# Block-sparse attention and token mix on one core: the middle value block of a window copied on chip instead of loaded

## The chip, the cores and the metric

The kernel runs on one core of one Trainium2 chip. The metric is the device time of one execution in microseconds (us). A measurement is the median of several runs.

## What is computed

The reference is a block-sparse attention followed by a mixing block. There are 4 batches of 8 heads, 768 positions and 64 values per head; positions are grouped in 24 blocks of 32. Each query block sees its own block and both neighbours, the first and the last block, and three sampled blocks. The first and the last query block see everything.

```python
scores = scale * np.matmul(q, k.transpose(0, 1, 3, 2))
mask = np.abs(blk_i - blk_j) <= window                       # window = 1 block
mask = mask | (blk_i == 0) | (blk_j == 0) | (blk_i == n_blocks - 1) | (blk_j == n_blocks - 1)
for qb in range(n_blocks):
    for kb in sampled_blocks[qb]:
        mask[qb * block:(qb + 1) * block, kb * block:(kb + 1) * block] = True
scores = np.where(mask, scores, -1000000000.0)
attn = np.exp(scores - np.max(scores, axis=-1, keepdims=True))
attn = attn / (np.sum(attn, axis=-1, keepdims=True) + 1e-09)
x = np.matmul(attn, v)                                       # heads side by side: (4, 768, 512)
...
theta = x @ w_theta
yr = np.einsum('ts,bsd->btd', w_tok_r, x * np.cos(theta))
yi = np.einsum('ts,bsd->btd', w_tok_i, x * np.sin(theta))
u = x + yr + yi
return u + np.maximum(u @ w_ch, 0.0)
```

The weights of the mixing block come as 64-bit floats. The kernel decodes them on chip into a high and a low 32-bit part.

## The kernel before

**Two stages.** `attention` comes first and stores its result in device memory (`xs`); `token_mix` reads it back and does the rest. Only a little of the second stage starts inside the first.

**Units.** Attention works on two pairs of batches (`bp` 0 and 1). A pair has six units for its first and last query block (`"w"`, the edges, which see all keys) and then 22 inner units, `i` = 1 to 22, one for each other query block: 56 units in a row, and step `n` of one loop treats several of them at different ages. The order inside a step is written out by hand (lines 483 to 519), and each engine takes its instructions in that order:

- `scores` of unit n+1 on TensorE (`S`, line 333), its row minimum on VectorE (`m`, line 336), the exponentials on ScalarE (`weights`, `P`, line 353);
- `gather_window` and `gather_keys` of unit n+3 on GpSimd: they copy the key blocks that this unit sees into one of two buffers `kg` (lines 293 and 272). A buffer is free when the scores two units earlier are done;
- a share of the decoding of the weights on VectorE and ScalarE (`Decoder`); how many shares a step gets is `due`;
- `turn` and `evict` of unit n (`T`, `pT`), `values` of unit n-1 on TensorE (`X`, line 387), `finish` of unit n-1 on VectorE;
- on SyncE's queue the query load of unit n+6, the window's values of unit n+1 (`load_window`, line 301), the store of the result; on GpSimd the indirect gather of the sampled values of unit n+2 (`gather_values`, line 307); and the next pair's keys, 256 KB at a time.

**The values of a unit.** The product `X` of an inner unit reads two tiles of 128 rows by 1040 (32 rows for each block, all 16 heads of the pair with a column of ones). `va` holds the window: blocks i-1, i and i+1, block b in rows 32 (b mod 3) to 32 (b mod 3) + 31, and the first block in rows 96 to 127. `vb` holds the three sampled blocks, gathered by their row numbers, and the last block. There are two `va`, taken in turn by even and odd units, and four `vb`. Since a `va` was last filled two units ago, one of its three window blocks is still right, and `fresh(i)` lists the two others, i and i+1, as one load of 260 KB or, where they don't lie side by side, two of 130 KB:

```python
for b0, n in fresh(i):
    s0 = 32 * (b0 % 3)
    nc.sync.dma_start(va[s0 : s0 + 32 * n], vr[768 * bp + 32 * b0 : 768 * bp + 32 * (b0 + n)])
```

Block i of unit i also stands in the other `va`, where unit i-1 has it as its own i+1, in the same rows.

**Waits.** Instructions of different engines wait for each other by semaphores, which the framework sets from the tiles that they read and write. A queue is in order: what waits holds up all that stands behind it. In the rows of the order below, `PE_49`, `DVE_49`, `Activation_49` and `Pool_49` count the work of the engines, `DMAHW0` to `7` tell of the landing of transfers from SyncE's and ScalarE's queues, `DMASW0` to `7` of the landing of transfers from GpSimd's. GpSimd's indirect gathers take the eight DMASW semaphores in turn: the gather of unit 1 raises `DMASW0`, that of unit 6 `DMASW5`, that of unit 9 `DMASW0` again.

Of the kernel before, what the change touches and what calls it, by code (L numbers as in the profile page):

```python
# [14 lines left out]
AF = mybir.ActivationFunctionType  # L15
# [4 lines left out]
P = 128  # L20
# [23 lines left out]
class Piece:  # L44
# [6 lines left out]
    def __init__(self, nc, parts, src, name):  # L51
        self.nc, self.parts, self.src, self.name = nc, parts, src, name
        self.f = src.shape[1] // 2
# [73 lines left out]
class Tables:  # L127


    def __init__(self, nc, cp, sampled):  # L130
        self.raw = cp.tile([P, NB * 6], I32, name="sb_raw")
        nc.sync.dma_start(self.raw, sampled.rearrange("i k -> (i k)").partition_broadcast(P))

    def make(self, nc, cp):
        raw = self.raw
# [40 lines left out]
def attention(tc, qT, qE, kT, vr, sampled, xs, ident, early_pieces, late_pieces, first_place, follow, spares):  # L176
# [13 lines left out]
    nc = tc.nc  # L190
    with ExitStack() as ctx, ExitStack() as early:
# [11 lines left out]
        ps_t = ctx.enter_context(tc.tile_pool(name="ps_t", bufs=2, space=PSUM))  # L203
        ps_x = ctx.enter_context(tc.tile_pool(name="ps_x", bufs=2, space=PSUM))


        first = cp.tile([P, 1], F32, name="first")
        nc.vector.memset(first, 0.0)
        tc.keep_in_program_order(nc.scalar.activation(first, first, AF.Exp))
        kgs = [kgp.tile([P, 8, 8, 32], F32, name=f"kg{x}") for x in range(2)]  # L210
        vas = [gp.tile([P, 1040], F32, name=f"va{x}") for x in range(2)]
        vbs = [gp.tile([P, 1040], F32, name=f"vb{x}") for x in range(VB)]
        ks, wide, qbs, qes, unscaled, st, numbers = {}, {}, {}, {}, {}, {}, {}

        def make_places(bp):

            if bp == 0:
                place = first_place([P, 13824], F32, "kv0")
                k = place[:, 0:6144]
                wide[bp] = [place[:, 6144 + 1040 * c : 6144 + 1040 * (c + 1)] for c in range(6)]  # L220
            else:
                k = kp.tile([P, 6144], F32, name="k1")
                wide[bp] = vbs + vbs[:2]
            ks[bp] = k.rearrange("r (s g f) -> r s g f", s=NB, g=8)

        def load_k(bp, s0, n, queue=nc.sync):
            queue.dma_start(ks[bp][:, s0 : s0 + n].rearrange("r s g f -> r s (g f)"), kT[bp][:, s0 : s0 + n])

        def load_wide(bp, t, queue=nc.sync):
            for c in (2 * t, 2 * t + 1):  # L230
                queue.dma_start(wide[bp][c], vr[768 * bp + 128 * c : 768 * bp + 128 * c + 128])

        def load_q(bp, i):
            if i % 2 == 0:
                return
            t = qp.tile([P, 2, 2, 4, 32], F32, tag="q", name=f"q{bp}_{i}", bufs=Q_BUFS)
            nc.sync.dma_start(t.rearrange("r u b p f -> r u (b p f)"), qT[bp][:, i - 1 : i + 1, :])
            qbs[bp, i], qbs[bp, i + 1] = t[:, 0], t[:, 1]
            unscaled[bp, i] = t.rearrange("r u b p f -> r (u b p f)")
# [8 lines left out]
        def scale_edges(bp):  # L248
            scale(qes[bp].rearrange("r b p f -> r (b p f)"))

        def load_edges(bp):
            qes[bp] = ep.tile([P, 2, 4, 64], F32, tag="qe", name=f"qe{bp}")
            nc.sync.dma_start(qes[bp].rearrange("r b p f -> r (b p f)"), qE[bp])


        def number_blocks(bp, i):
# [21 lines left out]
        def fresh(i):  # L278

            runs = []  # L280
            for blk in range(i - 1 if i <= 2 else i, i + 2):
                if runs and blk % 3:
                    runs[-1][1] += 1
                else:
                    runs.append([blk, 1])
            return runs
# [6 lines left out]
                nc.gpsimd.tensor_copy(kgs[i % 2][:, s0 : s0 + n], ks[bp][:, b0 : b0 + n])  # L293

        def load_window(bp, i):
            va = vas[i % 2]
            if i <= 2:
                nc.sync.dma_start(va[96:128], vr[768 * bp : 768 * bp + 32])
            for b0, n in fresh(i):
                s0 = 32 * (b0 % 3)  # L300
                nc.sync.dma_start(va[s0 : s0 + 32 * n], vr[768 * bp + 32 * b0 : 768 * bp + 32 * (b0 + n)])

# [114 lines left out]
        def join(bp, a):  # L417

            xw, f = xws[a], fs[a].rearrange("r t (e b) -> r t b e", e=2)
            for t in range(3):  # L420
                nc.gpsimd.tensor_tensor(xw[:, t], xw[:, t], f[:, t].unsqueeze(3).to_broadcast([P, 2, 2, 65]), op=ALU.mult)
            nc.gpsimd.tensor_tensor(xw[:, 0], xw[:, 0], xw[:, 1], op=ALU.add)
            nc.gpsimd.tensor_tensor(xw[:, 0], xw[:, 0], xw[:, 2], op=ALU.add)

        def joined(bp, a):
            xe = wp.tile([P, 2, 2, 2, 64], F32, tag="xo", name=f"xe{bp}_{a}", bufs=2)[:, 0]
            normalised(f"{bp}_a{a}", xws[a][:, 0], xe)
            for s_ in range(2):
                for z in range(2):
                    r0, p0 = 64 * s_ + 32 * z, 32 * (2 * a + s_)  # L430
                    nc.sync.dma_start(xs[bp, p0 : p0 + 32, (NB - 1) * z].rearrange("r b c -> r (b c)"), xe[r0 : r0 + 32].rearrange("r b e d -> r (b e d)"))

        mxs, fs, xws, xos = {}, {}, {}, {}
        units = []
        for bp in range(NP):
            units += [(bp, "w", (t, a)) for t in range(3) for a in range(2)] + [(bp, i, None) for i in range(1, NB - 1)]
        half = len(units) // 2
# [5 lines left out]
        def do(n, stage, *args):  # L443
            if 0 <= n < len(units):
                stage(units[n], *args)

        def inner(n, stage):
            if 0 <= n < len(units) and units[n][1] != "w":
                stage(*units[n][:2])
# [4 lines left out]
        spares.append(lambda: qp.tile([P, 4, 4, 32], F32, tag="q", name=f"spare{len(spares)}", bufs=Q_BUFS))  # L454
        with tc.manual_schedule():
            tab = Tables(nc, cp, sampled)
            load_edges(0)
            make_places(0)
            load_k(0, 0, 8)
            tab.make(nc, cp)  # L460
            load_wide(0, 0)
            decoder = Decoder(early_pieces + late_pieces, stage, nc.scalar)
            for t in range(1, 3):
                load_k(0, 8 * t, 8)
                load_wide(0, t)
                decoder.load(t - 1, nc.sync)
                load_q(0, 2 * t - 1)
            make_places(1)
            scale_edges(0)
            do(0, scores)  # L470
            do(0, weights)
            steps = len(units) + 1
            for n in range(steps):
                if n == len(units) - 1:
                    early_s.close()
                    next(follow)

                if n <= half:
                    due = 3 * len(early_pieces) * max(n - 3, 0) // (half - 3)
                else:  # L480
                    due = 3 * len(early_pieces) + 3 * len(late_pieces) * (n - half) // (len(units) - 4 - half)
                due = min(due, 3 * len(decoder.pieces)) - decoder.at
                decoder.first_on_scalar(due)
                do(n + 1, scores)
                inner(n + 4, number_blocks)
                inner(n + 3, gather_window)
                inner(n + 3, gather_keys)
                if due > 0:
                    decoder.on_vector()
                if due > 1 and decoder.at % 3:  # L490
                    decoder.on_vector()
                do(n, turn)
                do(n - 1, values)
                if len(units) - 2 <= n < len(units):
                    next(follow)
                do(n, evict)
                do(n + 1, weights)
                inner(n + 3, gather_key)
                inner(n + 3, scale_q)
                decoder.on_scalar()  # L500
                do(n - 1, finish)
                if units[min(n + 6, steps - 2)][:2] not in ((0, 1), (0, 3)):
                    inner(n + 6, load_q)
                inner(n + 1, load_window)
                inner(n - 1, store)
                inner(n + 2, gather_values)
                if 0 < n <= len(units) and units[n - 1][1:] in (("w", (2, 0)), ("w", (2, 1))):
                    join(units[n - 1][0], units[n - 1][2][1])
                if 1 < n <= len(units) and units[n - 2][1:] in (("w", (2, 0)), ("w", (2, 1))):
                    joined(units[n - 2][0], units[n - 2][2][1])  # L510
                if 8 <= n < 20:
                    load_k(1, 2 * (n - 8), 2)
                if n == 24:
                    load_edges(1)
                if n == half - 3:
                    scale_edges(1)
                for t, step in enumerate((half - 2, half, half + 2)):
                    if n == step:
                        load_wide(1, t)

                if n == len(units) - 4:
                    early.close()
                if len(units) - 6 <= n < len(units):
                    next(follow)
            assert not decoder.left(), decoder.left()
# [394 lines left out]
```

## Time and profile before

| | |
|---|---|
| time, median of 3 runs | 618.04 us (616.56 to 621.01) |
| the profiled execution: its time, its span | 618.49 us, 616.7 us |
| granted TensorE clock | 0.955 |
| busy: TensorE, VectorE, ScalarE, GpSimd | 550.4, 413.6, 335.6, 142.1 us |
| moved by DMA | 90.40 MB, mean 147 GB/s |
| GpSimd's gathers of `vb` | 44, issue 1.0 us each, 7.5 us (median) from issue to landing |

In the rows of the profile PE is TensorE, PEld its weight loads, DVE VectorE, ACT ScalarE, POOL GpSimd, SP SyncE; a q behind the name is the engine's queue for transfers and waits. A group's row gives line, engine, operation, out<-in, shape and count, then busy time in us, mean ns of one, and behind the second bar the engine's idle time just before, with what ended it. A row of a window gives, behind its bounds and length, the busy us (and count) of PE, PEld, DVE, ACT and POOL, then the granted clock, the share of time that the 16 DMA engines were busy, and GB/s. A row of the timeline gives start and length in us. The 40 slices of the page are 15.4 us each; a digit is a tenth.

### The profile page before, as it was taken

The numbers are of one execution on the slowest core, as the hardware profiler recorded it, in microseconds if no ns is written. First come the engines' busy times: TensorE is split into PE (matmuls) and PEld (weight loads), VectorE is DVE, ScalarE is ACT, GpSimd is POOL, SyncE is SP. The second block draws the span as 40 slices with busy tenths as digits, with TensorE's granted clock in tenths as the row PEclk, the third lists the DMA queues.
The fourth block names the chain that finished last, engine by engine and source line by source line (L and its number), as shares of the span: only waits on it lengthen the run. The fifth ranks groups of instructions, "written<-read, shape, count | busy, mean of one in ns | idle before, by whom it ended". The sixth has DMA issues, their size and how long they took to land.

```text
span 616.7 us, 17251 instructions
## 1 busy us (share of the span) xinstructions
PE 550.4 (89%) x7072; PEld 438.2 (71%) x7072; DVE 413.6 (67%) x845; ACT 335.6 (54%) x684; POOL 142.1 (23%) x252
## 2 busy tenths in 40 slices
PE   4986759779886886899999997999999999999997
PEld 2755536556654564678888886888888888888886
DVE  5696558679988676777999997446842648723252
ACT  3887468669877676874656645144640346520220
POOL 1496336460584453521101000000000000000000
PEclk9998798899889889899999999999999999999999
DMA  8969899888989899763342222311112210112002
GB/s 321 333 166 263 235 283 264 240 234 299 264 216 279 209 260 247 189 163 119 88 108 81 71 83 78 106 41 35 57 46 78 78 51 21 37 39 78 1 0 103
DMA packets 54095, 90.40 MB, mean 147 GB/s; under 512 B 5504, under 2 KB 31744, under 8 KB 53632
## 3 DMA queue, kind: packets, MB, share of 16 engines
q1 hardware_dynamic: 44480, 58.07, 31.0%
q0 software_dynamic: 6688, 21.78, 13.7%
q10 hardware_dynamic: 2848, 9.44, 5.4%
q8 instruction: 56, 0.92, 0.7%
q14 instruction: 23, 0.19, 0.1%
HBM read 76.68 MB, written 12.58 MB: 145 GB/s over the span
## 4 chain that ended last, share of the span: by engine, by line
PE 56%; DMA 15%; DVE 13%; ACT 6%; issue 5%; POOL 2%; SPq 1%; POOLq 0%; DVEq 0%; ACTq 0%
PE ya L648 14%; DMA va<-in_vr_dram 11%; PE yb L648 7%; PE X L387 6%; PE S L333 4%; PE T L363 4%; PE o L675 3%; PE o L676 2%; PE o L677 2%; PE h L589 2%; PE h L592 2%; PE h L590 2%; ACT zh L630 2%; PE T_w L363 1%; DMA vb<-in_vr_dram 1%
## 5 line engine op out<-in xcount | busy, mean ns | idle before, releaser
L648 PE MATMUL ya<-w_second,zh 128*128 128x512 f32 x288 | 107.1, 396 | 0.0
L648 PE MATMUL yb<-w_second,zh 128*128 128x256 f32 x288 | 80.5, 279 | 0.0
L353 ACT ACTIVATE P<-S,m 128x256 f32<-128x256 f32 x176 | 69.9, 497 | 10.3 <-DVE m L336 10.1
L333 PE MATMUL S<-kg,q 64*32 64x256 f32 x1408 | 59.0, 422 | 17.6 <-issue 14.9
L387 PE MATMUL X<-va,pT 128*32 128x65 f32 (+1 forms) x1408 | 53.3, 241 | 23.4 <-DMA va<-in_vr_dram 17.3
L369 ACT COPY pT<-T 128x512 f32<-128x512 f32 x88 | 48.1, 598 | 45.4 <-PE T L363 44.9
L336 DVE TENSOR_REDUCE m<-S 128x4 f32<-128x1024 f32 x44 | 53.7, 1220 | 28.0 <-PE S L333 27.5
L363 PEld LDWEIGHTS T<-ident,P 128*128 128x128 f32 x352 | 43.7, 155 | 34.1 <-ACT P L353 15.7
L648 PEld LDWEIGHTS ya<-w_second,zh 128*128 128x128 f32 x288 | 54.1, 188 | 14.0
L363 PE MATMUL T<-ident,P 128*128 128x128 f32 x352 | 58.8, 308 | 4.3 <-ACT P L353 3.8
L387 PEld LDWEIGHTS X<-va,pT 128*32 128x32 f32 (+1 forms) x1408 | 38.1, 121 | 33.5 <-issue 16.8
L648 PE MATMUL ya<-w_second,zl 128*128 128x512 f32 x144 | 58.0, 403 | 0.0
L387 PE MATMUL X<-vb,pT 128*32 128x65 f32 (+1 forms) x1408 | 52.7, 240 | 2.6 <-issue 2.6
L648 PEld LDWEIGHTS yb<-w_second,zh 128*128 128x128 f32 x288 | 54.4, 189 | 0.4
L307 POOL DMA_INDIRECT vb<-in_vr_dram,rows x44 | 44.7, 1017 | 30.4 <-PE X_w L387 22.3
L333 PEld LDWEIGHTS S<-kg,q 64*32 64x32 f32 x1408 | 23.8, 114 | 28.6 <-issue 18.2
L387 PEld LDWEIGHTS X<-vb,pT 128*32 128x32 f32 (+1 forms) x1408 | 40.1, 123 | 3.1 <-issue 3.1
L605 DVE SCALAR_TENSOR_TENSOR rr<-t,h 128x512 f32<-128x512 f32 x24 | 16.5, 687 | 37.8 <-ACT t L599 37.8
L648 PE MATMUL yb<-w_second,zl 128*128 128x256 f32 x144 | 40.9, 284 | 0.0
L589 PE MATMUL h<-w_theta_hi,xh 128*128 128x512 f32 x96 | 38.3, 398 | 0.4 <-ACT xh L578 0.4
L683 DVE SCALAR_TENSOR_TENSOR of<-o,xT 128x512 f32<-128x512 f32 (+1 forms) x24 | 13.3, 557 | 36.7 <-PE o L677 33.7
L590 PE MATMUL h<-w_theta_lo,xh 128*128 128x512 f32 x96 | 37.9, 394 | 0.0
(166 smaller groups left out, 1262.9 us busy)
## 6 DMA issues: line engine op xcount, KB each, us to landing
va<-in_vr_dram SPq DMA_DIRECT2D x30, 260.0 KB
q<-in_qT_dram SPq DMA_DIRECT2D x22, 256.0 KB
xs<-xo SPq DMA_DIRECT2D x22, 256.0 KB
xr<-xs SPq DMA_DIRECT2D x22, 256.0 KB
xa<-xs SPq DMA_DIRECT2D x88, 64.0 KB
raw_tok_r<-in_w_tok_r_dram ACTq DMA_DIRECT2D x8, 576.0 KB
out_dram<-of SPq DMA_DIRECT2D x16, 256.0 KB
va<-in_vr_dram SPq DMA_DIRECT2D x30, 130.0 KB
```

The lines of the kernel that those rows point to most:

```text
L307: nc.gpsimd.indirect_dma_start(out=vb[0:96], out_offset=None, in_=vr, in_offset=bass.IndirectOffsetOnAxis(ap=tab.rows[:, bp, i : i + 1], a ...
L333: nc.tensor.matmul(sc[32 * p : 32 * p + 32, e, b, :], q[rows, b, p, :], keys[rows, :, 4 * b + p, :], start=True, stop=True)
L336: nc.vector.tensor_reduce(m.rearrange("r (e b) -> r e b", e=2), sc, axis=AX.X, op=ALU.min)
L353: nc.scalar.activation(pt[:, e, b], sc[:, e, b], AF.Exp, bias=m[:, 2 * e + b : 2 * e + b + 1], scale=-1.0)
L363: nc.tensor.transpose(banks[k // 4][:, k % 4], pt[:, (k // 2) % 2, k % 2, 128 * (k // 4) : 128 * (k // 4) + 128], ident)
L369: nc.scalar.copy(out[:, 4 * h : 4 * h + 4], bank)
L387: nc.tensor.matmul(s["X"][rr, b, e, :], s["T"][0:rows, 4 * c + 2 * e + b, rr], v[0:rows, v0 : v0 + 65], start=c == 0, stop=c == 1,)
L589: nc.tensor.matmul(ps, hi[:, c, :], wh[:, c, :], start=c == 0, stop=False)
L590: nc.tensor.matmul(ps, hi[:, c, :], wl[:, c, :], start=False, stop=False)
L605: nc.vector.scalar_tensor_tensor(r, t, -C1, ps, op0=ALU.mult, op1=ALU.add)
L648: nc.tensor.matmul(acc, z[:, dd], wt[:, t0 : t0 + n], start=first and (n == 512 or c % 2 == 0), stop=last, skip_group_check=n == 256,)
L675: nc.tensor.matmul(ps, wh, uh, start=first, stop=False, skip_group_check=one)
```

## The change

Four things are edited.

1. `load_window`: from unit 3 of a pair on, block i is copied by GpSimd from the other `va` (32 rows by 1040), and only block i+1 is loaded, 130 KB. `gather_values` now stands ahead of `load_window` in the step.
2. The second pair's keys: the same 12 loads of 256 KB, one in every second step from 5 to 27 instead of one in every step from 8 to 19.
3. The decoding in the second half: the six steps after `half` (the second pair's edges) get 4 parts of weight, later steps 7, instead of all the same.
4. At the start, the block numbers and the edge queries are loaded by ScalarE's queue instead of SyncE's, and the first exponential, which brings in its table, stands behind them.

```diff
     def __init__(self, nc, cp, sampled):
         self.raw = cp.tile([P, NB * 6], I32, name="sb_raw")
-        nc.sync.dma_start(self.raw, sampled.rearrange("i k -> (i k)").partition_broadcast(P))
+        nc.scalar.dma_start(self.raw, sampled.rearrange("i k -> (i k)").partition_broadcast(P))
...
         first = cp.tile([P, 1], F32, name="first")
-        nc.vector.memset(first, 0.0)
-        tc.keep_in_program_order(nc.scalar.activation(first, first, AF.Exp))
...
-        def load_edges(bp):
+        def load_edges(bp, queue=nc.sync):
             qes[bp] = ep.tile([P, 2, 4, 64], F32, tag="qe", name=f"qe{bp}")
-            nc.sync.dma_start(qes[bp].rearrange("r b p f -> r (b p f)"), qE[bp])
+            queue.dma_start(qes[bp].rearrange("r b p f -> r (b p f)"), qE[bp])
...
         def load_window(bp, i):
-            va = vas[i % 2]
+            va, runs = vas[i % 2], fresh(i)
             if i <= 2:
                 nc.sync.dma_start(va[96:128], vr[768 * bp : 768 * bp + 32])
-            for b0, n in fresh(i):
+            else:
+
+                runs, slot = [(i + 1, 1)], slice(32 * (i % 3), 32 * (i % 3) + 32)
+                nc.gpsimd.tensor_copy(va[slot], vas[(i + 1) % 2][slot])
+            for b0, n in runs:
                 s0 = 32 * (b0 % 3)
                 nc.sync.dma_start(va[s0 : s0 + 32 * n], vr[768 * bp + 32 * b0 : 768 * bp + 32 * (b0 + n)])
...
             tab = Tables(nc, cp, sampled)
-            load_edges(0)
+            load_edges(0, nc.scalar)
             make_places(0)
             load_k(0, 0, 8)
+
+            nc.vector.memset(first, 0.0)
+            nc.scalar.activation(first, first, AF.Exp)
             tab.make(nc, cp)
...
                 if n <= half:
                     due = 3 * len(early_pieces) * max(n - 3, 0) // (half - 3)
                 else:
-                    due = 3 * len(early_pieces) + 3 * len(late_pieces) * (n - half) // (len(units) - 4 - half)
+
+                    weight = lambda k: 4 * min(k, 6) + 7 * max(k - 6, 0)
+                    due = 3 * len(early_pieces) + 3 * len(late_pieces) * weight(n - half) // weight(len(units) - 4 - half)
...
+                inner(n + 2, gather_values)
                 inner(n + 1, load_window)
                 inner(n - 1, store)
-                inner(n + 2, gather_values)
...
-                if 8 <= n < 20:
-                    load_k(1, 2 * (n - 8), 2)
+                if 5 <= n < 29 and n % 2:
+                    load_k(1, n - 5, 2)
```

How instructions stand on GpSimd, in the steps that gather the values of units 4 to 6 of the first pair. Before (line 307 is the gather, 293 and 272 the key copies):

```order
L307 DMA vb1_121<-in_vr_dram,rows_160 96x1040
L258 TENSOR_LOAD sb_block_136
L293 COPY kg0_116<-kv0_130 128x512 [waits PE_49]
...
L272 COPY kg0_116<-kv0_130 128x256
L307 DMA vb2_122<-in_vr_dram,rows_160 96x1040 [waits DMASW0_49]
L258 TENSOR_LOAD sb_block_136
L293 COPY kg1_117<-kv0_130 128x512 [waits PE_49,Pool_49]
...
L272 COPY kg1_117<-kv0_130 128x256 [waits Pool_49]
L307 DMA vb3_123<-in_vr_dram,rows_160 96x1040 [waits DMASW1_49]
```

And in the change (line 308 is the gather, 299 the new copy, 290 and 269 the key copies):

```order
L308 DMA vb1_119<-in_vr_dram,rows_160 96x1040
L299 COPY va1_117<-va0_116 32x1040 [waits DMAHW3_49,DMAHW1_49,PE_49]
L255 TENSOR_LOAD sb_block_136
L290 COPY kg0_114<-kv0_128 128x512 [waits PE_49]
...
L269 COPY kg0_114<-kv0_128 128x256
L308 DMA vb2_120<-in_vr_dram,rows_160 96x1040 [waits DMASW0_49]
L299 COPY va0_116<-va1_117 32x1040 [waits DMASW3_49,DMASW4_49,DMASW2_49,DMAHW0_49,DMASW1_49,DMAHW7_49,PE_49,Pool_49]
L255 TENSOR_LOAD sb_block_136
L290 COPY kg1_115<-kv0_128 128x512 [waits PE_49,Pool_49]
...
L269 COPY kg1_115<-kv0_128 128x256
L308 DMA vb3_121<-in_vr_dram,rows_160 96x1040
L299 COPY va1_117<-va0_116 32x1040 [waits DMASW5_49,DMAHW7_49,PE_49,Pool_49]
```

Between a gather and the next key copies there is now a copy. The three shown are those of units 3, 4 and 5, whose blocks lie in rows 0, 32 and 64. Each waits for a product on TensorE (`PE_49`) and the landing of the other `va` (`DMAHW`). Those of units 4 and 5 wait for gathers as well: unit 5's for `DMASW5`, which the gather just ahead of it raises, unit 4's for `DMASW1` to `4`, the last of which is the gather just ahead. The same pattern repeats every three units in both pairs: rows 0 without a DMASW wait, rows 32 and 64 with one.

On SyncE, the window's loads of units 5 to 7 (`va1` is the odd units' buffer). Before:

```order
L301 DMA va1_119<-in_vr_dram 32x1040 [waits DMAHW0_49,PE_49]
L301 DMA va1_119<-in_vr_dram 32x1040 [waits DMAHW1_49]
L227 DMA k1_188<-in_kT_dram 128x512 [waits DMAHW2_49]
L237 DMA q0_11_1036<-in_qT_dram 128x512 [waits DMAHW3_49,Activation_49]
L301 DMA va0_118<-in_vr_dram 64x1040 [waits DMAHW5_49,PE_49]
L415 DMA xs_73<-xo0_3_938 128x512 [waits DMAHW6_49,DVE_49]
L227 DMA k1_188<-in_kT_dram 128x512 [waits DMAHW7_49]
L301 DMA va1_119<-in_vr_dram 64x1040 [waits DMAHW0_49,PE_49]
```

And in the change:

```order
L302 DMA va1_117<-in_vr_dram 32x1040 [waits DMAHW1_49,PE_49,Pool_49]
L224 DMA k1_188<-in_kT_dram 128x512 [waits DMAHW2_49]
L234 DMA q0_11_1039<-in_qT_dram 128x512 [waits DMAHW3_49,Activation_49]
L302 DMA va0_116<-in_vr_dram 32x1040 [waits DMAHW5_49,PE_49,Pool_49]
L416 DMA xs_73<-xo0_3_941 128x512 [waits DMAHW6_49,DVE_49]
L302 DMA va1_117<-in_vr_dram 32x1040 [waits DMAHW7_49,PE_49,Pool_49]
```

Each unit has one load of 32 rows now, one of the key loads has gone to another step, and the window's load waits for GpSimd too: for the copy that filled the same rows two units earlier.

## The prediction

> **What bounds the kernel now.** I read the page's slices first, then the windows by stage, then the groups with what ended their idle time, and last the tile that carries the gathered values.
>
> ```profile
> PE   4986759779886886899999997999999999999997
> POOL 1496336460584453521101000000000000000000
> DMA  8969899888989899763342222311112210112002
> 45.00:60.00 15.00, 10.13 (x235) 7.26 (x236) 11.39 (x21) 12.13 (x30) 11.12 (x17) 0.87 1.00 266
> 75.00:90.00 15.00, 11.08 (x332) 7.28 (x316) 10.23 (x21) 12.04 (x29) 7.16 (x13) 1.00 1.00 282
> 400.00:616.00 216.00, 212.58 (x1160) 182.71 (x1158) 108.41 (x204) 74.10 (x114) 0.00 (x0) 1.00 0.15 48
> L387 PE MATMUL X<-va,pT 128*32 128x65 f32 (+1 forms) x1408 | 53.3, 241 | 23.4 <-DMA va<-in_vr_dram 17.3
> ```
>
> There are two programs in one span. From about 275 us on, the token mix keeps TensorE busy (212.58 of 216 us) and the DMA engines nearly idle (0.15); nothing of the change lies there, so that part only moves to where attention ends. In attention it is the other way round: in the two windows the DMA engines are busy all the time (1.00, at 266 and 282 GB/s), TensorE 10 to 11 of 15 us, and its idle time before the window's products is ended mostly by the landing of `va`. GpSimd has about half of its time free. The change takes bytes from the crowded engines and gives work and, as the built order shows, waits to GpSimd's queue. So the question is whether that queue stays off the path.
>
> ```profile
> 47.10 0.92 POOL L307 DMA_INDIRECT vb<-in_vr_dram,rows  x1 [0.16 <-issue]
> 144.23 0.26 PE L387 MATMUL X<-va,pT 128*32 128x65 f32 x4
> ...
> 180.08 1.25 POOL L307 DMA_INDIRECT vb<-in_vr_dram,rows  x1 [0.16 <-issue]
> 274.54 0.26 PE L387 MATMUL X<-va,pT 128*32 128x65 f32 x4
> ...
> 47.10:144.20 97.10, 73.03 (x1946) 51.48 (x1944) 64.38 (x122) 65.21 (x153) 46.51 (x82) 0.88 0.91 253
> POOL kg L293 <- PE S L333: 39.3, 15, 6.2
> ```
>
> These rows are the yardstick. The gather for unit 5 is issued at 47.10 us in the first pair and at 180.08 us in the second; the last unit's value product (unit 22) starts at 144.23 and 274.54 us. The stretches last 97.1 and 94.5 us, 191.6 us together. In the first one GpSimd works 46.5 us, and its idle time is 39.3 us of waiting for TensorE's score products: TensorE leads, GpSimd follows.
>
> **The change part by part.** *Bytes removed.* Forty units (3 to 22 of both pairs) no longer load their middle block.
>
> ```profile
> va<-in_vr_dram SPq DMA_DIRECT2D x30, 260.0 KB
> va<-in_vr_dram SPq DMA_DIRECT2D x30, 130.0 KB
> ```
>
> A block is 130 KB, so 40 x 133,000 bytes = 5.3 MB go. At 266 GB/s that is 20 us of a saturated DMA. It is an upper bound: it counts only while the DMA engines are what is waited for.
>
> *Copies added.* Forty copies of 32 rows by 1040 elements on GpSimd. The nearest rows are its key copies.
>
> ```profile
> L293 POOL COPY kg<-kv 128x512 f32<-128x512 f32 x15 | 9.4, 627 | 26.8 <-PE S L333 26.8
> L293 POOL COPY kg<-kv 128x768 f32<-128x768 f32 x1 | 0.8, 823 | 5.9 <-DVE sb_raw L163 5.9
> ...
> 93.60 0.61 POOL L293 COPY kg<-kv 128x512 f32<-128x512 f32 x1 [5.82 <-PE S L333]
> 94.16 0.74 POOL L272 COPY kg<-kv 128x256 f32 x2
> 95.05 0.96 POOL L307 DMA_INDIRECT vb<-in_vr_dram,rows  x1 [0.15 <-issue]
> ```
>
> 256 more elements in a row cost 0.2 us, so 1040 cost 0.82 + 272 x 0.2/256 = 1.03 us; with the 0.15 us between two GpSimd instructions, 1.2 us. The bounds are 1.0 and 2.1 us (twice, if VectorE gets in its way). From the first key copy to the gather's issue a step takes 1.45 us (93.60 to 95.05), up to 2 us in crowded steps; I take 1.5. The issue itself takes 0.95 us. Without any wait a step of GpSimd would be 1.5 + 0.95 + 1.2 = 3.65 us against 97.1 / 18 = 5.4 us of the pipeline today: hidden.
>
> *The wait added.* This decides. The built order shows that a copy whose slot is at rows 32 or 64 (13 of 20 units in each pair) waits for the landing semaphore of gathers that GpSimd issued before it; for 12 of the 13 that includes the one issued immediately before. Copies into rows 0 to 31 don't. The copy also stands behind the gather in the queue now. So GpSimd issues the gather, stands still until its 390 KB have landed, copies, and only then starts the key copies of two units later and the next gather. Before, it went straight on. What such a landing takes:
>
> ```profile
> DMA to landing us min/median/max: 4.7/7.5/11.6
> DMA to landing us min/median/max: 6.8/9.6/11.6
> DMA to landing us min/median/max: 4.7/5.3/6.2
> DMA to landing us min/median/max: 5.0/5.1/7.6
> 118.00:135.00 17.00, 14.33 (x418) 10.54 (x417) 13.50 (x26) 12.81 (x30) 11.03 (x19) 0.91 0.83 242
> 200.00:233.00 33.00, 27.71 (x744) 19.18 (x735) 24.25 (x47) 23.61 (x56) 16.80 (x31) 0.85 0.88 236
> ```
>
> The four landing rows are of tile `vb`: all gathers, then those of 46 to 62 us (DMA share 1.00), 118 to 135 us and 200 to 233 us, whose shares (0.83 and 0.88) stand below. From issue to landing it is never under 4.7 us, 5.1 to 5.3 where the DMA engines have some air, and 9.6 where they have none. In the changed kernel the same stretch carries 5.3 MB less and lasts longer, so they have air; but the key, query and store transfers of the step go out just when the gather does. Call the landing L; I take 5.6 us, with 4.7 and 7.5 as bounds.
>
> *The sum.* From the gather of unit 5 to the last copy of a pair GpSimd's queue holds: 12 landings that are waited out and a last one before the copy of unit 22, 13 L; 18 copies outside the landings, 18 x 1.2 = 21.6; 16 stretches of key copies, 16 x 1.5 = 24; 5 gathers that nobody waits for, 5 x 0.95 = 4.8. That is 13 L + 50.4, at L = 5.6 us 123.2 us. TensorE's 73 us and the DMA traffic fit beside it, so the queue is the path. Two pairs: 246.4 - 191.6 = +54.8 us. The copy of unit 3 stands before the stretch in each pair: +2.4.
>
> The Trainium skill, page "DMA: Bandwidth & Descriptors", section "Anatomy of one DMA — SWDGE (gpsimd) path", fits such a transfer as 2.0 us plus bytes over 436 GB/s: an estimate of 2.9 us for 399,360 bytes. By it a pair would be 13 x 2.9 + 50.4 = 88 us, less than today's 97, and the wait would cost nothing. No gather in this trace was that fast.
>
> *Smaller parts.* Three thirds of a decoded piece leave the six edge steps of the second pair, where VectorE is nearly full.
>
> ```profile
> 160.00:180.00 20.00, 15.82 (x362) 11.02 (x354) 18.25 (x28) 14.03 (x35) 17.14 (x27) 0.89 0.88 223
> L75 DVE TENSOR_SCALAR ds_tok_r<-da_tok_r 128x576 int32<-128x576 int32 x8 | 5.4, 678 | 0.1
> L77 DVE SCALAR_TENSOR_TENSOR raw_tok_r<-raw_tok_r,ds_tok_r 128x576 f32<-128x576 uint32 x8 | 7.1, 887 | 0.3
> 0.75 0.39 SPq L132 DMA_DIRECT2D sb_raw<-in_sampled_dram  x1
> 1.65 0.43 SPq L227 DMA_DIRECT2D kv<-in_kT_dram  x1
> ```
>
> One third is 0.68 + 0.89 = 1.6 us, three are 4.7; I take -3 (bounds 0 and -4.7), since part lies beside GpSimd's joins. They come back in later steps, under the waits. At the start two transfers go to ScalarE's queue, so SyncE's first key load starts up to 0.9 us earlier; the table load behind them waits for the edge queries anyhow: -0.5 (0 to -0.9). The second pair's keys, 12 loads of 256 KB over 24 steps instead of 12, cost nothing: the last is issued four steps before its use, and each step's share of SyncE's queue gets shorter, not longer. If a step shrank to 3 us the last would still have 12 us. Moving `vb`'s small SyncE loads ahead of `va`'s touches four units of a pair: nothing.
>
> The profiled execution took 618.5 us (span 616.7, and 1.8 around it), 0.5 over the median of 618.0. 618.5 + 54.8 + 2.4 - 3 - 0.5 = 672 us. The half microsecond to the median is far inside the range.
>
> **The rivals.** *The bytes win.* If the waits stayed inside today's idle time of GpSimd, TensorE would find `va` earlier: 618.5 - 20 x 0.9 - 3.5 = 597 us, with 0.9 for the DMA share in the stretch. It needs a pair of units to shrink by 9 us, so 13 L + 50.4 under some 88 us and L under 2.9 us. For it: the DMA share of 1.00 and the 17.3 us waits for `va`. Against it: 4.7 us as the fastest landing. By the skill's fit just named it would happen; the trace does not agree (4.7 to 11.6). Chance 0.06.
>
> *Nothing measurable.* L at about 3.7 us would make a pair 98.5 us, as long as now, and 617 us in all; also where the wait is met early because something else holds the copy just as long. The same minimum speaks against it. Chance 0.04.
>
> *The landings stay as slow as today.* GpSimd's gather then collides with the step's own burst each time, L = 7.5: 2 x 13 x 1.9 = 49 us more, 721 us. For it: the bursts are tied to the same event as the gather. Against: 40 fewer blocks and a longer stretch leave the DMA engines busy some 0.6 of the time (0.9 x 191.6 = 172 us of work less 20, over 246). Chance 0.14.
>
> **How the numbers follow.** The forecast, 672 us, has 0.76. L from 4.7 to 7.2 us alone gives 649 to 714; the small parts and a dearer copy widen it a little: 645 to 715 us. Below lie the first two rivals, above most of the third. About 1% is what a measurement of this kernel can tell from no change. Slower by over 1%: 0.76 + 0.14 = 0.90; within 1%: 0.04; faster by over 1%: 0.06.
>
> **What would show it.** Right: GpSimd's copy of `va` as the largest wait on that engine, ended by the landing of `vb`, some 26 times for 4 to 5 us each; units in a rhythm of two long steps (about 8 us) and a short one (under 4); DMA share in attention near 0.6; TensorE waiting for GpSimd where it waited for `va`; attention ending near 328 us; the token mix unchanged in length. Copies near 1.03 us. Wrong: copies that start right behind the gather's issue, or TensorE still waiting for `va`'s landing. If landings last under 4 us, the term 13 L is mis-sized; if copies take 2 us, the other.

## The result and the profile after

Slower by a tenth. The changed kernel takes 681.34 us (median of 4 runs, 676.56 to 684.5) beside 617.3 us for the kernel before (4 runs, 615.27 to 621.01); the ratio is 1.102 [1.094, 1.111]. The profiled execution is the fastest of the four: 676.56 us, span 674.8, 58.1 us more than the profiled one of before. By the page its granted TensorE clock is 0.921.

The slices and two group rows of the changed kernel's page come first.

```profile
PE   3976766766987576556999999899999999999997
POOL 1394464463376555554600000000000000000000
DMA  8956656656888564646434322221121211102002
L388 PE MATMUL X<-va,pT 128*32 128x65 f32 (+1 forms) x1408 | 55.8, 255 | 80.1 <-POOL va L299 76.4
L299 POOL COPY va<-va 32x1040 f32<-32x1040 f32 x40 | 44.1, 1101 | 110.7 <-DMA vb<-in_vr_dram,rows 95.4
```

In the third line the DMA digits of attention, 8 and 9 before, are mostly 5 and 6 now. The value products (L388) stood idle 23.4 us before, mostly for a transfer; now 80.1 us, 76.4 of them for GpSimd's new copy, so the bytes of `va` are no longer what they wait for. The copy itself (L299) is busy 44.1 us and has 110.7 us of idle time ahead of it, 95.4 of it ended by the landing of `vb`. The row of the waits gives total us, how many, and the longest one, and the row of the tile `vb` the landings.

```profile
POOL va L299 <- DMA vb<-in_vr_dram,rows: 95.4, 22, 6.6
DMA to landing us min/median/max: 4.3/4.8/11.3
```

GpSimd's timeline in the changed kernel shows one period of three units: start, length, and in brackets the idle time before.

```profile
79.98 0.93 POOL L308 DMA_INDIRECT vb<-in_vr_dram,rows  x1
84.66 1.55 POOL L299 COPY va<-va 32x1040 f32<-32x1040 f32 x1 [3.75 <-DMA vb<-in_vr_dram,rows]
86.26 0.74 POOL L290 COPY kg<-kv 128x256 f32<-128x256 f32 x2
86.94 0.74 POOL L269 COPY kg<-kv 128x256 f32 x2
87.84 0.94 POOL L308 DMA_INDIRECT vb<-in_vr_dram,rows  x1
88.78 1.06 POOL L299 COPY va<-va 32x1040 f32<-32x1040 f32 x1
89.78 0.61 POOL L290 COPY kg<-kv 128x512 f32<-128x512 f32 x1
90.33 0.73 POOL L269 COPY kg<-kv 128x256 f32 x2
91.22 0.95 POOL L308 DMA_INDIRECT vb<-in_vr_dram,rows  x1 [0.16 <-issue]
97.03 1.04 POOL L299 COPY va<-va 32x1040 f32<-32x1040 f32 x1 [4.85 <-DMA vb<-in_vr_dram,rows]
```

The copy at 88.78 fills rows 0 to 31 and starts the moment the gather has been issued (87.84 + 0.94). Those at 84.66 and 97.03 go to rows 64 and 32 and stand 3.75 and 4.85 us until the gather just ahead has landed; key copies and the next gather stand behind them.

The two stretches of the yardstick (gather of unit 5 to the last unit's value product) in the changed kernel's timeline and windows:

```profile
51.34 0.93 POOL L308 DMA_INDIRECT vb<-in_vr_dram,rows  x1 [0.16 <-issue]
172.17 0.26 PE L388 MATMUL X<-va,pT 128*32 128x65 f32 x4
207.86 0.99 POOL L308 DMA_INDIRECT vb<-in_vr_dram,rows  x1 [0.16 <-issue]
331.83 0.26 PE L388 MATMUL X<-va,pT 128*32 128x65 f32 x4
51.34:172.20 120.86, 82.31 (x1950) 57.42 (x1949) 64.03 (x122) 65.42 (x153) 60.97 (x92) 0.77 0.63 180
207.86:331.80 123.94, 82.92 (x1936) 58.07 (x1936) 74.20 (x151) 70.74 (x162) 63.52 (x94) 0.81 0.55 154
```

They last 120.8 and 124.0 us where they lasted 97.1 and 94.5. The 58.1 us of the profiled pair split up as follows: start to the first gather of the yardstick 47.10 to 51.34, +4.2; first stretch +23.7; between the stretches 35.85 to 35.69, -0.2; second stretch +29.5; from its end to the span's end 342.2 to 343.0 (616.7 - 274.54, 674.8 - 331.83), +0.8. The token mix only begins later.

### The profile page after: what moved, and what is told of

It is laid out like the page before. It is cut to its first block, busy times and chain, and to the rows that moved or that the text cites. A ratio compares the mean times of both kernels' runs of the same rounds, so it can differ in the third digit from the quotient of the medians.

```text
span 674.8 us, 17347 instructions
## 1 busy us (share of the span) xinstructions
PE 564.4 (84%) x7072; PEld 446.8 (66%) x7072; DVE 414.1 (61%) x845; ACT 335.5 (50%) x684; POOL 182.4 (27%) x292
## 4 chain that ended last, share of the span: by engine, by line
PE 39%; DMA 21%; DVE 12%; POOL 11%; issue 7%; ACT 5%; POOLq 3%; SPq 0%; DVEq 0%
DMA vb<-in_vr_dram,rows 18%; PE ya L654 13%; PE yb L654 7%; POOL kg L269 3%; POOLq L255 3%; POOL kg L290 3%; POOL va L299 3%; PE o L681 2%; PE o L682 2%; PE h L595 2%; PE o L683 2%; PE h L596 2%; PE h L598 2%; ACT zh L636 2%; PE S_w L326 1%
## 5 line engine op out<-in xcount | busy, mean ns | idle before, releaser
L388 PE MATMUL X<-va,pT 128*32 128x65 f32 (+1 forms) x1408 | 55.8, 255 | 80.1 <-POOL va L299 76.4
L388 PEld LDWEIGHTS X<-va,pT 128*32 128x32 f32 (+1 forms) x1408 | 38.1, 129 | 90.5 <-POOL va L299 82.9
L299 POOL COPY va<-va 32x1040 f32<-32x1040 f32 x40 | 44.1, 1101 | 110.7 <-DMA vb<-in_vr_dram,rows 95.4
L334 PE MATMUL S<-kg,q 64*32 64x256 f32 x1408 | 65.2, 490 | 5.4 <-POOL kg L269 4.7
L364 PEld LDWEIGHTS T<-ident,P 128*128 128x128 f32 x352 | 46.2, 163 | 30.8 <-issue 16.7
L654 PEld LDWEIGHTS ya<-w_second,zh 128*128 128x128 f32 x288 | 54.1, 188 | 14.0
L388 PE MATMUL X<-vb,pT 128*32 128x65 f32 (+1 forms) x1408 | 56.1, 255 | 0.3 <-issue 0.3
L395 DVE TENSOR_SCALAR sm<-X 128x4 f32<-128x4 f32 x44 | 7.0, 159 | 73.3 <-PE X L388 73.1
L308 POOL DMA_INDIRECT vb<-in_vr_dram,rows x44 | 43.1, 979 | 16.2 <-PE X_w L388 9.3
L388 PEld LDWEIGHTS X<-vb,pT 128*32 128x32 f32 (+1 forms) x1408 | 41.0, 133 | 0.5 <-issue 0.5
L334 PEld LDWEIGHTS S<-kg,q 64*32 64x32 f32 x1408 | 25.4, 129 | 23.3 <-issue 11.7
```

Of the source, the lines that this page charges most:

```text
L299: nc.gpsimd.tensor_copy(va[slot], vas[(i + 1) % 2][slot])
L308: nc.gpsimd.indirect_dma_start(out=vb[0:96], out_offset=None, in_=vr, in_offset=bass.IndirectOffsetOnAxis(ap=tab.rows[:, bp, i : i + 1], a ...
L334: nc.tensor.matmul(sc[32 * p : 32 * p + 32, e, b, :], q[rows, b, p, :], keys[rows, :, 4 * b + p, :], start=True, stop=True)
L364: nc.tensor.transpose(banks[k // 4][:, k % 4], pt[:, (k // 2) % 2, k % 2, 128 * (k // 4) : 128 * (k // 4) + 128], ident)
L388: nc.tensor.matmul(s["X"][rr, b, e, :], s["T"][0:rows, 4 * c + 2 * e + b, rr], v[0:rows, v0 : v0 + 65], start=c == 0, stop=c == 1,)
L654: nc.tensor.matmul(acc, z[:, dd], wt[:, t0 : t0 + n], start=first and (n == 512 or c % 2 == 0), stop=last, skip_group_check=n == 256,)
```

## Experiments

Two theories stood against each other on the loss. The *landing* theory is the prediction's: a copy of GpSimd into rows 32 or 64 waits for gathers in flight, and that wait is the path. The *copy* theory says that 40 more copies in GpSimd's queue, and products that wait for them, cost it. Later runs ask how much the bytes alone bring and what the start costs. Ratios are to the kernel before on the same chip, with 95% intervals.

**No copy at all.** The middle block is loaded again, as before the change; all else is the change's.

```diff
-            else:
-                runs, slot = [(i + 1, 1)], slice(32 * (i % 3), 32 * (i % 3) + 32)
-                nc.gpsimd.tensor_copy(va[slot], vas[(i + 1) % 2][slot])
```

> Both fresh blocks are loaded again; the other three edits of the change and the place of the gather ahead of the window's load stay. Theory (GpSimd's queue stands still at copies that wait for gathers, and nothing else costs much): back to about 620 us, 617 to 624, the first value product still 3 us later than before because of the start, GpSimd's waits for vb gone. Rival (the respread key loads, the decoding shares or the gather's place cost the most): 640 us or more, attention still ending later than 320 us.

Measured: 618.21 us, 1.0057 [1.002, 1.0095]. With the copy goes nearly the whole loss, although the 5.3 MB are moved again; the order of the gather, the key loads' new steps, the decoding and the start cost at most some 6 us together (0.2 to 0.95%). The waits of this run:

```profile
POOL kg L290 <- PE S L330: 76.7, 32, 7.5
```

GpSimd waits for TensorE's score products again, as before the change. This doesn't part copy from wait; the next ones do.

**The gather behind the copy.** The copies and their waits stay, but the gather just ahead isn't in flight yet.

```diff
-                inner(n + 2, gather_values)
                 inner(n + 1, load_window)
                 inner(n - 1, store)
+                inner(n + 2, gather_values)
```

> The copy stays on GpSimd with its waits, but the gather is issued behind the copy again, so a copy waits for the gather issued one step earlier. Theory: the key copies (1.5 us) and the issue now lie inside the landing, so a waiting step takes about L + 1.35 = 6.2 us instead of L + 2.65 = 7.5, in all 24 x 1.3 = 31 us less: about 647 us, 635 to 658. Rival (the copy's own length and its wait for va set the pace, not the gather's landing): unchanged, 672 to 685 us.

Measured: 643.36 us, 1.048 [1.040, 1.057], as the landing theory had it (647, 635 to 658). The waits of GpSimd's copy, and a stretch of its timeline:

```profile
POOL va L299 <- DMA vb<-in_vr_dram,rows: 50.3, 18, 4.7
81.81 0.94 POOL L308 DMA_INDIRECT vb<-in_vr_dram,rows  x1 [0.16 <-issue]
82.75 0.62 POOL L290 COPY kg<-kv 128x512 f32<-128x512 f32 x1
83.30 0.73 POOL L269 COPY kg<-kv 128x256 f32 x2
85.90 1.05 POOL L299 COPY va<-va 32x1040 f32<-32x1040 f32 x1 [1.86 <-DMA vb<-in_vr_dram,rows]
87.22 0.92 POOL L308 DMA_INDIRECT vb<-in_vr_dram,rows  x1 [0.27 <-POOL va L299]
```

The copy still waits for the gather before it, but that one was issued a step earlier, and the key copies of 1.3 us lie inside its landing. The waits fall from 95.4 to 50.3 us and the loss from 64 to 27 us beside the kernel before. The same 40 copies are there, so their number alone isn't it.

**Copies into rows 0 to 31 only.** 14 of the 40 stay on GpSimd, none of them with a wait for a gather; the other units load the block as before.

```diff
-            else:
+            elif i % 3 == 0:
```

> GpSimd copies only where the slot is rows 0 to 31 (7 of 20 units in a pair), which has no wait for gathers; the other units load both blocks. Theory (the wait, not the copy): 612 to 621 us, near the kernel without copies, with 1.9 MB less moved. Rival (a copy on GpSimd costs as such): 14 of 40 copies, a third of the slowdown, 635 to 645 us.

Measured: 610.94 us, 0.990 [0.987, 0.993]: faster than before by about 1%, and 1 us below the range of the theory (612 to 621).

```profile
L299 POOL COPY va<-va 32x1040 f32<-32x1040 f32 x14 | 14.8, 1059 | 26.5 <-DMA va<-in_vr_dram 18.0 <-PE X L388 7.0 <-PE T L364 1.5
```

Each copy takes 1.06 us, as in the change, but no landing of `vb` is among what ends its idle time. By the copy theory 14 copies should have kept 14/40 of the loss, about 22 us; there is none. As the cause of the whole loss, the copy theory falls.

**A thin copy.** GpSimd copies 16 elements of a row instead of 1040; the wait stays.

```diff
-                nc.gpsimd.tensor_copy(va[slot], vas[(i + 1) % 2][slot])
+                nc.gpsimd.tensor_copy(va[slot, 0:16], vas[(i + 1) % 2][slot, 0:16])
```

> The copy moves 16 of its 1040 columns and keeps all its waits; the rest of the middle block is left as it was, so the result is not the reference's. Theory (GpSimd's queue is the path, and its sum is 13 landings plus copies plus key copies): each of some 18 copies of a pair outside a landing gets about 0.9 us shorter, 30 to 36 us less than the change, 642 to 652 us. Rival (the landing alone sets the pace and the copy lies beside other work): 672 to 685 us.

Measured: 657.87 us, 1.065 [1.059, 1.072], between the two expectations.

```profile
L299 POOL COPY va<-va 32x16 f32<-32x16 f32 x40 | 10.0, 249 | 117.7 <-DMA vb<-in_vr_dram,rows 89.4 <-DMA q<-in_qT_dram 11.3 <-PE T L364 11.1
POOL kg L290 <- PE X L388: 7.3, 15, 0.6
```

The wait for landings is nearly whole (89.4 beside 95.4 us) and so is most of the loss: 40 us of 64 with hardly any copying. The copies' own time is the rest: 0.85 us less each, for the 36 that the sum has outside the landings, makes 30.6 us, of which about 23.5 came out. The difference fits the second row, 7.3 us in which key copies now wait for TensorE, but no run tests that. So wait and copies lie one behind the other in one queue, as the sum had them, and the wait is the larger part.

**The copy on another engine.** First ScalarE, then VectorE; the bytes are saved as in the change, and neither copy waits for a gather.

```diff
-                nc.gpsimd.tensor_copy(va[slot], vas[(i + 1) % 2][slot])
+                nc.scalar.copy(va[slot], vas[(i + 1) % 2][slot])
```

```diff
-                nc.gpsimd.tensor_copy(va[slot], vas[(i + 1) % 2][slot])
+                nc.vector.tensor_copy(va[slot], vas[(i + 1) % 2][slot])
```

> The same copy on ScalarE, which is given no wait for gathers; everything else as in the change. Theory: without that wait the 5.3 MB that are saved show, less what 40 copies of about 1 us cost on ScalarE, which has 65 of 97 us busy: 600 to 630 us. Rival (any engine that copies must wait for the other buffer's landing, and that wait is what costs): 650 us or more, ScalarE's largest wait being the landing of va.

> The same copy on VectorE, without a wait for gathers; everything else as in the change. Theory: 598 to 628 us, the copy 0.6 to 1.2 us long, GpSimd again waiting for score products. Rival (the wait for the other buffer costs, whoever copies): 650 us or more, VectorE's row minimum late behind the copy.

Measured: on ScalarE 610.66 us, 0.991 [0.988, 0.995]; on VectorE 614.94 us, 0.998 [0.995, 1.002]. The copies' row of ScalarE's run, what TensorE's transposes wait for there and in VectorE's run, and a window of ScalarE's:

```profile
L299 ACT COPY va<-va 32x1040 f32<-32x1040 f32 x40 | 42.2, 1056 | 3.3 <-DMA va<-in_vr_dram 2.7
...
PEld T L364 <- ACT P L354: 46.0, 115, 1.9
PEld T L364 <- ACT P L354: 54.1, 118, 2.4
...
49.00:139.80 90.80, 75.74 (x1972) 49.69 (x1956) 66.79 (x128) 87.44 (x177) 43.39 (x77) 0.94 0.87 245
```

Forty copies of the same length on ScalarE (1.06 us) cost nothing net; only their wait and their place in GpSimd's queue made them dear. But the saved bytes bring 6 us beside the kernel before and 7.6 beside the run that loads the block again, not 20. In the window ScalarE is busy 87.4 of 90.8 us, and TensorE's transposes wait 46.0 us for its exponentials (15.7 us before; 54.1 with the copy on VectorE). On VectorE the bytes bring nothing that can be told from no change. That the exponentials take up the saved bytes is argued from these waits; the versions with the copy shared out test it below.

**The old start.** With the block loaded again, then with the better copies, the block numbers and the edge queries go back to SyncE's queue and the first exponential to the very beginning.

```diff
-        nc.scalar.dma_start(self.raw, sampled.rearrange("i k -> (i k)").partition_broadcast(P))
+        nc.sync.dma_start(self.raw, sampled.rearrange("i k -> (i k)").partition_broadcast(P))
...
-            load_edges(0, nc.scalar)
+            load_edges(0)
```

> Both fresh blocks loaded, and the block numbers and edge queries back on SyncE's queue ahead of the keys, the first exponential first on ScalarE; only the respread keys, the decoding shares and the gather's place are left of the change. Theory (the edge queries share the DMA engines with the key and value loads when they come from another queue, 3 us at the start): first value product at 17.1 us again, 3 us less than with the new start, about 615 us, 612 to 617. Rival (later waits take the 3 us up): 617 to 620 us, as with the new start.

Measured: 616.07 us, 1.0003 [0.997, 1.003], beside 1.0057 [1.002, 1.0095] with the new start: the intervals touch. The profiles are clearer. The edge queries' scaling, the first score products and the first window products, in the changed kernel and then in the kernel before:

```profile
9.37 0.63 ACT L239 ACTIVATE qe<-qe 128x512 f32<-128x512 f32 x1 [6.21 <-DMA qe<-in_qE_dram]
10.05 3.69 PE L326 MATMUL S_w<-kv,qe 64*64 64x256 f32 x32 [10.05 <-ACT qe L239]
20.22 0.98 PE L388 MATMUL X_w<-kv,pT_w 128*64 128x65 f32 x26
...
5.44 0.63 ACT L242 ACTIVATE qe<-qe 128x512 f32<-128x512 f32 x1 [3.19 <-DMA qe<-in_qE_dram]
8.15 3.69 PE L325 MATMUL S_w<-kv,qe 64*64 64x256 f32 x32 [8.15 <-DMA kv<-in_kT_dram]
17.10 1.09 PE L387 MATMUL X_w<-kv,pT_w 128*64 128x65 f32 x30
```

From ScalarE's queue the edge queries are there 4 us later, TensorE waits for them instead of the keys, and the window products start 3.1 us later. With the old start they begin at 17.04 us here.

> The copy on ScalarE, without waits for gathers, and the old start. Theory: the gains of both add, 610.7 - 3 = about 607.5 us, 604 to 610. Rival (the start is taken up by later waits): 609 to 612 us.

> GpSimd copies rows 0 to 31 only, the other units load both blocks, and the old start. Theory (as with the ScalarE copy, the 3 us of the start are taken up later): 608 to 612 us, the same as with the new start. Rival (the gains add): 606 to 608.5 us.

Measured: the copy on ScalarE with the old start 610.03 us, 0.989 [0.986, 0.993] (0.991 without); 14 copies on GpSimd with the old start 609.03 us, 0.985 [0.981, 0.990] (0.990 without). Both lower, each by less than its interval; the first expectation, that the gains add (604 to 610), is just missed, and so is the second one's rival (606 to 608.5). In a profile the start is worth 3 us; in the time it is no more than about that, and not told apart from nothing.

**The copy shared out.** Rows 0 on GpSimd, rows 32 and 64 on ScalarE, or one third each on GpSimd, ScalarE and VectorE; both with the old start.

```diff
+                copy = nc.scalar.copy if i % 3 else nc.gpsimd.tensor_copy
+                copy(va[slot], vas[(i + 1) % 2][slot])
```

```diff
+                copy = nc.scalar.copy if i % 3 == 1 else nc.vector.tensor_copy if i % 3 == 2 else nc.gpsimd.tensor_copy
+                copy(va[slot], vas[(i + 1) % 2][slot])
```

> All forty copies, none with a wait for gathers: rows 0 to 31 on GpSimd, the others on ScalarE; old start. Theory (ScalarE, 87 of 91 us busy in a pair's stretch when it makes all copies, took up the saved bytes): ScalarE has 7 copies fewer per pair, about 7 us, so 603 to 608 us. Rival (the saved bytes are no longer waited for): 609 to 612 us as with all copies on ScalarE.

> All forty copies, none with a wait for gathers: rows 0 to 31 on GpSimd, 32 to 63 on ScalarE, 64 to 95 on VectorE; old start. Theory: no engine gets more than 7 us in a pair's stretch of 90, so most of the saved bytes show: 600 to 606 us. Rival: 609 to 612 us.

Measured: 610.21 us, 0.987 [0.983, 0.991], and 608.71 us, 0.984 [0.980, 0.989]. Both miss what was expected (603 to 608, 600 to 606). Waits of the kernel before, of 14 copies with the old start, of GpSimd with ScalarE, and of the run that loads every block again with the old start:

```profile
PE X L387 <- DMA va<-in_vr_dram: 17.3, 12, 3.6
PEld X L387 <- issue: 19.9, 39, 3.8
PEld T L363 <- ACT P L353: 15.7, 38, 2.1
...
PE X L390 <- DMA va<-in_vr_dram: 7.2, 7, 1.6
PEld X L390 <- issue: 31.4, 54, 2.6
PEld T L366 <- ACT P L356: 14.6, 38, 1.7
...
PE X L391 <- DMA va<-in_vr_dram: 2.3, 1, 2.3
PEld X L391 <- issue: 24.3, 63, 3.2
PEld T L367 <- ACT P L357: 21.8, 58, 1.4
...
PE X L386 <- DMA va<-in_vr_dram: 16.3, 8, 5.0
PEld X L386 <- issue: 34.4, 46, 5.2
```

The wait for `va` that the bytes could remove is 17.3 us (16.3 in the last run, 10.1 in the one without a copy and with the new start); 1.9 MB less (14 blocks) brings it to 7.2 and all 5.3 MB to 2.3. The waits for ScalarE's exponentials rise to 21.8 us with the copy on GpSimd and ScalarE, but not with 14 copies (14.6), and relieving ScalarE of copies gains nothing that can be told from its interval; so the exponentials alone don't explain the limit. Idle time of TensorE called issue, which ends on nothing that the profile shows, doesn't either: 31.4 and 24.3 us before these weight loads beside 19.9, but 34.4 in the run that saves no bytes. The three versions without a wait for gathers (14 copies, two engines, three engines, all with the old start) come to the same 609 to 610 us. They beat the kernel before by 1.3 to 1.6%, and no run tells them apart. What holds them there stays open.

## Why the prediction was right

The mechanism was the one forecast, and its sum came out close: 672 us beside 676.6 for the profiled execution and 681.3 for the median, inside the range. Part of the closeness is luck, as the pieces below show. The medians lie 64 us apart and the profiled pair 58.1; a trace can account only for the latter.

- *The wait and its place.* Expected: some 26 waits of 4 to 5 us on GpSimd's copy, ended by the landing of `vb`. The trace has them, in the rhythm of two stops and one straight run that the period above shows. The row of the waits puts 22 of them down to the landing, 4.3 us each (95.4 / 22) and 6.6 at most; the idle time of the other four has another releaser named. Two of these four are the last copies of the pairs, which TensorE's transposes release, so the thirteenth "landing" of each pair is not shown as one. Removing the copy, moving only the gather, and keeping only the copies that don't wait settle it between them.
- *The landing, L = 5.6.* The gather's issue to the start of the waiting copy measures 5.36 us on average in the first stretch and 5.50 in the second. The forecast that the DMA engines would have air held (shares 0.63 and 0.55, "near 0.6" expected), though the median landing on the tile is 4.8 us. Why the copies start later than that (a mean of 26 beside a median of 44) is not shown.
- *Copies and key copies.* 1.10 us each beside 1.03, and 1.55 to 1.59 us from the copy's end to the next gather beside 1.5. The two stretches together measure 244.8 us beside 246.4. Here two errors cancel: the landings were put some 4.5 us too long in all (26 times 0.17), and from the end of a pair's last copy to the last product pass 1.9 and 2.4 us, for which the sum had nothing. The thin copy checks the form of the sum from the other side: what leaves the queue comes out of the time, less what is then spent waiting for TensorE.
- *The rivals.* "The bytes win" needed landings under 2.9 us. The fastest of the 44 took 4.3. Where the wait is absent the bytes do win, but 6 to 10 us rather than 21 (and on VectorE nothing clear of noise), so that rival's price was too high as well: it took the whole share of the DMA engines for waiting time, and only the 17.3 us of waits for `va` were such. "As slow as today" needed 7.5 us and had 5.4 to 5.5.
- *The start, wrong in sign.* -0.5 was forecast; the first window products start 3.1 us later. The step that failed reads "the table load behind them waits for the edge queries anyhow". It looked at the seat that becomes free in SyncE's queue, not at the place that the small loads lose. They are issued as early as before (0.74 and 1.18 us beside 0.75 and 1.20), but the first key load now goes out at 0.74 us beside them instead of at 1.65 us behind them. That the shared DMA engines make them late is argued from this; no run changes the queue alone. The profiles show the lateness; the medians of the runs with the old start lean the same way, but their intervals overlap.
- *The edges of the decoding, too large.* -3 was forecast between the stretches, +1.2 for a copy. The profiled pair shows -0.2; in the run that loads the block again, with the old start, that piece is 33.8 us beside 35.85, and 34.5 in the one with the new start, so -1.3 to -2.1 for the decoding and what else changed there. Start, edges and end together came to +4.8 us in the profiled pair (4.2, -0.2 and 0.8) where -1.1 was forecast (2.4, -3 and -0.5). These 5.9 us are more than the 4.5 us by which the sum fell short of the profiled execution.
- *The second pair's keys.* Nothing was forecast and nothing stands out: the run that loads the block again, with the old start, keeps them and is at 1.0003.

The Trainium skill, page "DMA: Bandwidth & Descriptors", section "Anatomy of one DMA — SWDGE (gpsimd) path", gave an estimate of 2.9 us for such a gather. No trace here shows one that fast: the fastest landing that a view gives took 3.9 us (the run with the gather behind the copy), 4.3 in the changed kernel, where the DMA engines are busy 0.55 to 0.63 of the time. The measurement decides.

What stays open: why the waits for gathers come with copies into rows 32 and 64 and not into rows 0, and only on GpSimd. That they do is read from the built order and agrees with the runs above; why the framework sets them so is not shown.

## What to carry to other kernels

Before giving an engine a copy that saves bytes, read which semaphores that copy will wait for where it stands, and what is queued behind it on the engine: here the copy's 1.1 us was the small part, and a gather's landing, until then overlapped with the next step's work, became a stop in two of three steps. A transfer saved is worth at most the waits that it ends (10 to 17 us here), not its bytes over the bandwidth (20 us); at best 10 us came out in the time. A small load that is needed first should stand ahead of the big ones in the same queue: from another queue it went out beside them here and was there up to 4 us later.

## What the runs showed of the hardware

*TensorE's clock was lower behind its waits.* The same products took longer in the changed kernel: in the two stretches 165.2 us of TensorE's time beside 150.2 before, at granted clocks of 0.77 and 0.81 beside 0.88 and 0.86. TensorE's timeline around one wait for the copy, and windows of 2 us across it:

```profile
91.94 1.12 PE L334 MATMUL S<-kg,q 64*32 64x256 f32 x32
...
98.13 0.45 PE L388 MATMUL X<-va,pT 128*32 128x65 f32 x8 [4.04 <-POOL va L299]
...
100.02 1.96 PE L334 MATMUL S<-kg,q 64*32 64x256 f32 x32
...
92.00:94.00 2.00, 2.00 (x42) 1.37 (x40) 1.66 (x5) 2.00 (x7) 0.18 (x1) 1.00 0.58 149
100.00:102.00 2.00, 2.00 (x37) 0.76 (x34) 0.76 (x3) 0.00 (x0) 0.51 (x1) 0.50 0.49 81
```

Ahead of the stop that ends with 4.04 us of waiting for the copy the 32 score products of a unit take 1.12 us at a clock of 1.00; behind it 1.96 us at 0.50. This agrees with the Trainium skill, page "TensorE: Matmul & The Clock Gate", section "Part 1: The HAM clock gate (the "warmup" mystery)": after an idle window of about 3.4 us the array runs at half clock until it has been busy for as long. Here GpSimd hardly waits for the slower products: of its waits ahead of the copies only 4.7 of 110.7 us are ended by TensorE. With a shorter stop that might change.

*Small loads beside big ones.* The block numbers and the edge queries, issued at the very start from another queue, are used from 7.42 and 9.37 us on instead of 4.77 and 5.44. The page "DMA: Bandwidth & Descriptors" of the Trainium skill, section "Issuing engines are not separate DMA queues", says that such transfers interleave on the same engines and only issue time is saved. The rows fit that: the first key load is issued 0.9 us earlier, and the two small loads, now beside it, are used 2.7 and 3.9 us later.
